# Level products of two heads issued per head on half of the array's rows, with R kept without padding

## The chip, the cores and the metric

One core of a Trainium2 chip runs the whole kernel. The metric is the device time of one execution in microseconds (us), median of the runs. Ratios are the mean time of one kernel's runs over the mean of the other's runs of the same rounds, so they are not quite the ratio of the medians quoted beside them.

## The reference, cut to what matters

A linear recurrence with a decay per step and channel feeds a layer norm and an MLP. All is float32.

```python
# r, k, v, w: (4 batches, 8 heads, 768 steps, 48 channels)
for t in range(S):
    cur = einsum('bhd,bhe->bhde', u * k[t], v[t])
    y[t] = einsum('bhd,bhde->bhe', r[t], state + cur)
    state = w[t][..., None] * state + einsum('bhd,bhe->bhde', k[t], v[t])
x = y as (4, 768, 384)
out = x + relu(layer_norm(x) @ w1) @ w2        # w1: 384 x 1536, w2: 1536 x 384
```

## The kernel before

The steps are cut into 6 chunks of 128. Inside a chunk the weight of step s in step t is built in seven levels of block sizes n = 1, 2 .. 64. At each level A = K . R over the channels gives the entries whose s lies in the left and t in the right of two sibling blocks; then K and R are multiplied by the products T of whole blocks and go to the next level. A **unit** is a pair of heads of one batch; there are 16 units, so 112 levels. The two heads share the 128 partitions, 64 each, of which 48 carry data.

R is kept twice as wide as it need be: `R[(j, d), j', t]` is zero where j' is not the partition's own head j. So one product on all 128 rows gives both heads at once, side by side in 128 columns:

```python
for lev in range(NLEV):
    n = 1 << lev; nq = HP // n; last = lev == NLEV - 1; rows = n if last else P
    ...
    for c0 in range(0, NC, CB):                      # two banks of PSUM, three chunks each
        ps = ps_a.tile([P, CB, 2 * HP], F32, ...)
        for c in range(CB):
            PE.matmul(ps[0:rows, c, :]...,           # 128 weight columns (64 in the last level)
                      a["k"][:, ds((c0 + c) * P, rows)],
                      R[:, :, ds((c0 + c) * nq, nq), 1, :], start=True, stop=True)   # 128 moving
        # VectorE copies this half into A under a mask (ScalarE in the last level)
        DVE.copy_predicated(out=to, mask=mask, data=ps)
    POOL.tensor_tensor(out=K[:, :, 0, :], in0=K[:, :, 0, :], in1=T..., op=ALU.mult)
    for j in range(2):                               # R, one head after the other, 64 partitions
        rows = ds(HP * j, HP)
        if last:
            ACT.copy(out=rs[rows, :, 0, :], in_=R[rows, j, :, 0, :])
        DVE.tensor_tensor(out=rs[...] if last else R[rows, j, :, 1, :],
                          in0=R[rows, j, :, 1, :], in1=T[rows, ...], op=ALU.mult)
    yield
```

Unit q's levels are interleaved with the end of unit q - 1, the start of unit q + 1, the conversion of the MLP weights (24 steps, VectorE mostly, during the first 24 levels) and the MLP of the batch before. So there is no MLP work until five units, 35 levels, are nearly through. Which instruction goes where between these is settled when the program is built, by a scheduler that looks at dependencies.

## Time and profile before

| | before |
|---|---|
| time, median of the first 3 runs | 800.03 us (799.59 to 804.22) |
| TensorE busy | 704 us, 88% |
| VectorE busy | 457 us, 57% |
| a level beside the MLP, first record to the MLP's next | 1.34 us |
| distance of two levels with one MLP group between them | 5.21 us |

How to read it: busy time over the whole run mixes two stages. The page's 40 slices tell them apart; the chain that ended last then says whose work the end hung on. This is the head of the chain on the page before, shares of the span by engine:

```profile
PE 76%; DVE 15%; POOL 3%; issue 3%; ACT 1%; DMA 1%; SPq 1%; POOLq 0%; ACTq 0%; DVEq 0%
```

VectorE has 15% of it, nearly all in the first 230 us.

### The profile page before, as it was taken

How to read it: one execution, taken by the hardware profiler on the slowest of the kernel's cores; microseconds unless marked ns; L12 is line 12 of the kernel's file. 1: busy time of each engine (PE TensorE's matmuls, PEld its weight loads, DVE VectorE, ACT ScalarE, POOL GpSimd, SP SyncE). 2: the span in 40 equal slices, each digit the busy share in tenths (PEclk: the TensorE clock that was granted, in tenths of full speed). 3: DMA queues.
4: the chain of work that ended last, by engine and by line, in shares of the span. 5: the costliest groups of instructions: out<-in, count | busy, mean ns of one | idle time of the engine just before them, and what ended most of it. 6: DMA issues, size and time to landing. Idle time of an engine off the chain costs nothing.

```text
span 798.1 us, 9669 instructions
## 1 busy us (share of the span) xinstructions
PE 704.1 (88%) x3640; PEld 527.0 (66%) x3640; DVE 457.0 (57%) x791; ACT 191.5 (24%) x402; POOL 258.8 (32%) x329
## 2 busy tenths in 40 slices
PE   4446665677699999999999999999999999999998
PEld 3346565567577767776867777777777776655554
DVE  5699999988964656485645555686444643200000
ACT  3034151503223122321322032212230212020110
POOL 8646564554532314141423333333121110000000
PEclk9558585859999999999999999999999999999999
DMA  9667241402310102023202020110000000000000
GB/s 155 102 139 154 64 120 60 119 5 46 75 30 16 41 20 46 0 55 70 56 1 46 21 55 1 30 35 11 1 1 11 20 1 1 20 11 11 20 1 30
DMA packets 107855, 33.86 MB, mean 42 GB/s; under 512 B 101536, under 2 KB 104736, under 8 KB 107808
## 3 DMA queue, kind: packets, MB, share of 16 engines
q1 hardware_dynamic: 107808, 33.24, 19.7%
q8 instruction: 29, 0.48, 0.2%
q14 instruction: 18, 0.15, 0.1%
HBM read 28.51 MB, written 4.72 MB: 42 GB/s over the span
## 4 chain that ended last, share of the span: by engine, by line
PE 76%; DVE 15%; POOL 3%; issue 3%; ACT 1%; DMA 1%; SPq 1%; POOLq 0%; ACTq 0%; DVEq 0%
PE h_ps L390 24%; PE o_ps L400 23%; PE a_ps L269 18%; DVE R L293 5%; PE y L338 4%; DVE A L281 3%; PE y L343 2%; POOL tot L232 2%; PE kv L315 1%; DVE we L184 1%; DVE wm L188 1%; PE k_ps L210 1%; DVE we L176 1%; PE r_ps L210 1%; DVE wm L192 1%
## 5 line engine op out<-in xcount | busy, mean ns | idle before, releaser
L269 PE MATMUL a_ps<-R,kT 128*128 128x128 f32 (+1 forms) x1344 | 198.5, 304 | 75.2 <-DVE R L293 64.5
L269 PEld LDWEIGHTS a_ps<-R,kT 128*128 128x128 f32 (+1 forms) x1344 | 186.2, 206 | 106.2 <-issue 44.1
L281 DVE COPY_PREDICATED A<-mask,a_ps 128x384 f32<-128x384 int8 x192 | 135.2, 730 | 139.1 <-PE a_ps L269 133.0
L390 PE MATMUL h_ps<-xT,w_sb 128*128 128x384 f32 x576 | 195.3, 489 | 0.5 <-ACT xT L382 0.5
L400 PE MATMUL o_ps<-w_sb,h 128*128 128x384 f32 x576 | 193.1, 487 | 0.0
L282 POOL TENSOR_TENSOR kT<-kT,tot 128x384 f32<-128x384 f32 x96 | 92.0, 958 | 257.4 <-PE a_ps L269 257.4
L400 PEld LDWEIGHTS o_ps<-w_sb,h 128*128 128x128 f32 x576 | 106.5, 190 | 67.1 <-issue 0.9
L390 PEld LDWEIGHTS h_ps<-xT,w_sb 128*128 128x128 f32 x576 | 105.6, 190 | 65.6 <-ACT xT L382 1.7
L293 DVE TENSOR_TENSOR R<-R,tot 64x384 f32<-64x384 f32 x160 | 133.4, 833 | 2.2
L406 DVE TENSOR_TENSOR o<-o_ps,x 128x384 f32<-128x384 f32 x24 | 13.4, 557 | 156.6 <-PE o_ps L400 156.6
L395 ACT ACTIVATE h<-h_ps 128x384 f32<-128x384 f32 x96 | 47.0, 490 | 149.1 <-PE h_ps L390 149.0
L338 PE MATMUL y<-v,A 128*128 128x48 f32 x384 | 56.0, 278 | 0.0
L338 PEld LDWEIGHTS y<-v,A 128*128 128x128 f32 x384 | 54.0, 207 | 0.5
L220 ACT COPY R<-r_ps 64x384 f32<-64x384 f32 x64 | 30.2, 472 | 55.3 <-PE r_ps L210 54.2
L292 ACT COPY rs<-R 64x384 f32<-64x384 f32 x32 | 16.3, 509 | 108.4 <-DVE R L293 107.9
L238 POOL TENSOR_TENSOR rk<-nat_k,nat_r 128x576 f32<-128x576 f32 x16 | 24.4, 1526 | 42.0 <-DMA nat_r<-in_r_dram 42.0
L343 PE MATMUL y<-s,rs 128*128 128x96 f32 x160 | 37.0, 316 | 0.0
L282 POOL TENSOR_TENSOR kT<-kT,wT 128x384 f32<-128x384 f32 x16 | 19.7, 1233 | 47.3 <-PE a_ps L269 47.3
L195 POOL TENSOR_TENSOR w_sb<-wm,we 128x384 f32<-128x384 f32 x24 | 27.8, 1157 | 20.4 <-DVE wm L192 14.4
L180 ACT ACTIVATE we<-we,bias 128x384 f32<-128x384 int32 x24 | 14.8, 615 | 71.3 <-DVE we L176 71.3
L232 POOL TENSOR_TENSOR tot<-tot 128x192 f32<-128x192 f32 (+4 forms) x80 | 29.4, 368 | 5.7
L343 PEld LDWEIGHTS y<-s,rs 128*128 128x128 f32 x160 | 27.2, 213 | 0.0
(59 smaller groups left out, 523.7 us busy)
## 6 DMA issues: line engine op xcount, KB each, us to landing
raw<-in_moe_w_ch_dram SPq DMA_DIRECT2D x24, 384.0 KB, 3.4
nat_w<-in_w_dram SPq DMA_DIRECT2D x32, 144.0 KB, 3.0
nat_k<-in_k_dram SPq DMA_DIRECT2D x32, 144.0 KB, 2.9
nat_r<-in_r_dram SPq DMA_DIRECT2D x32, 144.0 KB, 3.1
v<-in_v_dram SPq DMA_DIRECT2D x32, 144.0 KB, 3.6
out_dram<-o SPq DMA_DIRECT2D x24, 192.0 KB, 1.8
u_bc<-in_u_dram SPq DMA_DIRECT2D x1, 192.0 KB, 3.6
g_sb<-in_moe_g_ln_dram SPq DMA_DIRECT2D x1, 1.5 KB, 3.1
```

The lines of the kernel that those rows point to most:

```text
L195: POOL.tensor_tensor(out=dst, in0=m, in1=e.bitcast(F32), op=ALU.mult)
L220: ACT.copy(out=a["r"][rows, j, cols], in_=ps[rows])
L232: POOL.tensor_tensor(out=t, in0=pair[:, :, 0], in1=pair[:, :, 1], op=ALU.mult)
L269: PE.matmul(ps[0:rows, c, :].rearrange("s (j q n) -> s j q n", j=2, n=n), a["k"][:, ds((c0 + c) * P, rows)], R[:, :, ds((c0 + c) * nq, nq) ...
L281: DVE.copy_predicated(out=to, mask=mask, data=ps)
L282: POOL.tensor_tensor(out=K[:, :, 0, :], in0=K[:, :, 0, :], in1=T[:, :, 1][:, :, None].broadcast_to([P, S // (2 * n), n]), op=ALU.mult,)
L293: DVE.tensor_tensor(out=rs[rows, :, 1, :] if last else R[rows, j, :, 1, :], in0=R[rows, j, :, 1, :], in1=T[rows, :, 0][:, :, None].broadca ...
L338: PE.matmul(y[:, i, ts(j, D)], a_bufs[q % 2][:, c, j, :], vs[b][:, c, 2 * g + j, :], start=i + j == 0, stop=c == 0, skip_group_check=True,)
L343: PE.matmul(y[:, i, :], a["rs"][:, ts(c, P)], s[:, c - 1, :], start=False, stop=True, skip_group_check=True,)
L390: PE.matmul(ps, w1_sb[:, kc, ts(f, P)], xT[:, kc, :], start=kc == 0, stop=kc == KC - 1,)
L395: ACT.activation(out=hs[f], in_=ps, func=AF.Relu)
L400: PE.matmul(ps, hs[f][:, ts(i, P)], w2_sb[:, f, :], start=f == 0, stop=f == FC - 1)
```

## The change

The intent: do not multiply zeros. R is stored once, `[128, 768]`; each head's product uses its own half of the array's rows (48 of them) and 64 moving columns, in the hope that two heads run side by side; and one VectorE instruction on 128 partitions updates R for both. The copies of R's even halves in the last level, and half of the copies that prepare R, go away. The diff, cut to its core (the rest is renamed tiles and removed comments):

```diff
-    r_bufs = [const.tile([P, 2, S], F32, name=f"R{i}") for i in range(2)]
...
-                if nm != "r":
-                    ACT.copy(out=a[nm][:, cols], in_=ps)
-                else:
-                    for j in range(2):
-                        rows = ds(HP * j, HP)
-                        ACT.copy(out=a["r"][rows, j, cols], in_=ps[rows])
+                ACT.copy(out=a[nm][:, cols], in_=ps)
...
-            for c0 in range(0, NC, CB):
-                ps = ps_a.tile([P, CB, 2 * HP], F32, tag="a", name=f"a_ps{q}_{lev}_{c0}")
-                for c in range(CB):
+            ps = [
+                ps_a.tile([P, NC, HP], F32, tag="a", name=f"a_ps{q}_{lev}_{j}") for j in range(2)
+            ]
+            for c in range(NC):
+                for j in range(2):
+                    head = ds(HP * j, D)
                     PE.matmul(
-                        ps[0:rows, c, :].rearrange("s (j q n) -> s j q n", j=2, n=n),
-                        a["k"][:, ds((c0 + c) * P, rows)],
-                        R[:, :, ds((c0 + c) * nq, nq), 1, :],
+                        ps[j][0:rows, c, :].rearrange("s (q n) -> s q n", n=n),
+                        a["k"][head, ds(c * P, rows)],
+                        R[head, ds(c * nq, nq), 1, :],
                         start=True, stop=True,
                     )
...
-            for j in range(2):
-                rows = ds(HP * j, HP)
-                if last:
-                    ACT.copy(out=rs[rows, :, 0, :], in_=R[rows, j, :, 0, :])
-                DVE.tensor_tensor(
-                    out=rs[rows, :, 1, :] if last else R[rows, j, :, 1, :],
-                    in0=R[rows, j, :, 1, :],
-                    in1=T[rows, :, 0][:, :, None].broadcast_to([HP, S // (2 * n), n]),
-                    op=ALU.mult,
-                )
+            DVE.tensor_tensor(
+                out=R[:, :, 1, :], in0=R[:, :, 1, :],
+                in1=T[:, :, 0][:, :, None].broadcast_to([P, S // (2 * n), n]), op=ALU.mult,
+            )
```

More of the change, by code (lines that the diff above doesn't have):

```diff
@@ L136 @@
     a_bufs = [const.tile([P, NC, 2, P], F32, name=f"A{i}") for i in range(2)]
-    r_bufs = [const.tile([P, 2, S], F32, name=f"R{i}") for i in range(2)]
     kv_buf = const.tile([P, NC - 1, 2, D], F32, name="kv_sb")
-    for t in (*r_bufs, *a_bufs, kv_buf):
+    for t in (*a_bufs, kv_buf):
         DVE.memset(t, 0.0)
@@ L202, in prep @@
         b, g = units[q]
-        a = st[q] = {"r": r_bufs[q % 2]}
+        a = st[q] = {}
         for nm in "wkr":
-            if nm != "r":
-                a[nm] = p2.tile([P, S], F32, tag=nm, name=f"{nm}T{q}")
+            pool = p3 if nm == "r" else p2
+            a[nm] = pool.tile([P, S], F32, tag=nm, name=f"{nm}T{q}")
             for c0 in range(0, NC, CB):
@@ L214, in prep @@
                 cols = ds(c0 * P, CB * P)
-                if nm != "r":
-                    ACT.copy(out=a[nm][:, cols], in_=ps)
-                else:
-                    for j in range(2):
-                        rows = ds(HP * j, HP)
-                        ACT.copy(out=a["r"][rows, j, cols], in_=ps[rows])
+                ACT.copy(out=a[nm][:, cols], in_=ps)
             yield
@@ L261, in levels @@
             rows = n if last else P
-            A = a_bufs[q % 2].rearrange("s c j (q two n) -> s (c j) q two n", two=2, n=n)
-            R = a["r"].rearrange("p j (q two n) -> p j q two n", two=2, n=n)
+            A = a_bufs[q % 2].rearrange("s c j (q two n) -> s c j q two n", two=2, n=n)
+            R = a["r"].rearrange("p (q two n) -> p q two n", two=2, n=n)
             K = a["k"].rearrange("p (q two n) -> p q two n", two=2, n=n)
             T = a["T"][lev].rearrange("p (q two) -> p q two", two=2)
-            for c0 in range(0, NC, CB):
-                ps = ps_a.tile([P, CB, 2 * HP], F32, tag="a", name=f"a_ps{q}_{lev}_{c0}")
-                for c in range(CB):
+            ps = [
[4 more added lines that the diff above has]
+                    head = ds(HP * j, D)
                     PE.matmul(
-                        ps[0:rows, c, :].rearrange("s (j q n) -> s j q n", j=2, n=n),
-                        a["k"][:, ds((c0 + c) * P, rows)],
-                        R[:, :, ds((c0 + c) * nq, nq), 1, :],
+                        ps[j][0:rows, c, :].rearrange("s (q n) -> s q n", n=n),
+                        a["k"][head, ds(c * P, rows)],
+                        R[head, ds(c * nq, nq), 1, :],
                         start=True, stop=True,
                     )
-                to = A[0:rows, ds(c0 * 2, CB * 2), :, 1, :]
-                ps = ps[0:rows].rearrange("s c (j q n) -> s (c j) q n", j=2, n=n)
+            for j in range(2):
+                to = A[0:rows, :, j, :, 1, :]
+                got = ps[j][0:rows].rearrange("s c (q n) -> s c q n", n=n)
                 if last:
-                    ACT.copy(out=to, in_=ps)
+                    ACT.copy(out=to, in_=got)
                 else:
-                    mask = masks[lev][:, None].broadcast_to([P, CB * 2, nq, n])
-                    DVE.copy_predicated(out=to, mask=mask, data=ps)
+                    mask = masks[lev][:, None].broadcast_to([P, NC, nq, n])
+                    DVE.copy_predicated(out=to, mask=mask, data=got)
             POOL.tensor_tensor(
@@ L285, in levels @@
             )
-            if last:
-                a["rs"] = p2.tile([P, S], F32, tag="rs", name=f"rs{q}", bufs=1)
-                rs = a["rs"].rearrange("p (q two n) -> p q two n", two=2, n=n)
-            for j in range(2):
-                rows = ds(HP * j, HP)
-                if last:
-                    ACT.copy(out=rs[rows, :, 0, :], in_=R[rows, j, :, 0, :])
-                DVE.tensor_tensor(
-                    out=rs[rows, :, 1, :] if last else R[rows, j, :, 1, :],
-                    in0=R[rows, j, :, 1, :],
-                    in1=T[rows, :, 0][:, :, None].broadcast_to([HP, S // (2 * n), n]),
-                    op=ALU.mult,
-                )
+            DVE.tensor_tensor(
+                out=R[:, :, 1, :], in0=R[:, :, 1, :],
+                in1=T[:, :, 0][:, :, None].broadcast_to([P, S // (2 * n), n]), op=ALU.mult,
+            )
             yield
@@ L343, in tail @@
                     PE.matmul(
-                        y[:, i, :], a["rs"][:, ts(c, P)], s[:, c - 1, :],
+                        y[:, i, :], a["r"][:, ts(c, P)], s[:, c - 1, :],
                         start=False, stop=True, skip_group_check=True,
```

## The prediction

> **What bounds the kernel now.** I read the 40 slices of the page first: the run has two regimes.
>
> ```profile
> PE   4446665677699999999999999999999999999998
> DVE  5699999988964656485645555686444643200000
> PEclk9558585859999999999999999999999999999999
> ```
>
> Each digit is a slice of 20 us. Until about 225 us (slice 11) VectorE is at nine tenths and TensorE at five, at a clock that is often half; from there to the end TensorE never rests and VectorE is half idle. The table of busy times by stretch puts numbers on it (columns: stretch, its length, busy time and count of each engine, granted clock, DMA share, GB/s):
>
> ```profile
> 59.20:229.00 169.80, 116.76 (x717) 105.60 (x717) 155.02 (x277) 54.35 (x113) 89.17 (x99) 0.77 0.35 80
> 229.00:699.00 470.00, 466.20 (x2509) 342.92 (x2507) 255.40 (x447) 107.47 (x231) 131.70 (x163) 1.00 0.10 24
> ```
>
> In the first row VectorE is busy 155 of 170 us; it also converts the MLP weights there, and there is no MLP yet to give TensorE. In the second TensorE is busy 466 of 470 us: whatever a level adds to TensorE there is paid in full, and whatever it saves on VectorE is worth nothing. The last 99 us are MLP alone and the change does not touch them. Counting the levels by their start, about 37 of the 112 (16 units of 7) start before 229 us, about 75 after it.
>
> The timeline of TensorE in the full stretch shows the price of two neighbouring levels (start, length, instruction; a float32 product is two recorded matmuls, so six products are x12):
>
> ```profile
> 408.50 1.50 PE L269 MATMUL a_ps<-R,kT 128*128 128x128 f32 x12
> 409.84 4.04 PE L390 MATMUL h_ps<-xT,w_sb 128*128 128x384 f32 x12
> 413.81 1.52 PE L269 MATMUL a_ps<-R,kT 128*64 128x128 f32 x12
> 415.26 0.91 PE L390 MATMUL h_ps<-xT,w_sb 128*128 128x384 f32 x2
> ```
>
> From start to start, the first level takes 409.84 - 408.50 = 1.34 us, 0.111 us a record: that is its place in the stream. The last level of a unit has 64 weight columns in place of 128 and is no cheaper: 415.26 - 413.81 = 1.45 us, and it starts 3.97 us after the MLP group ahead of it, of which 12 x 0.3225 = 3.87 us is streaming. I come back to that 0.10 us.
>
> What bounds a record with a narrow moving side is seen in the weight loads of the output products (48 moving columns):
>
> ```profile
> 306.26 0.97 PEld L338 LDWEIGHTS y<-v,A 128*128 128x128 f32 x8
> 307.15 0.30 PEld L343 LDWEIGHTS y<-s,rs 128*128 128x128 f32 x2
> ```
>
> Eight loads take (307.15 - 306.26) / 8 = 0.111 us each, as much as a record with 128 moving columns, although 48 columns stream in under half the time. So a record here costs the larger of its streaming (0.109 us at 128 columns) and its weight load (0.111 us for 128 weight columns). In the half-clock part the same loads come every 0.213 us.
>
> [...] The trace agrees on columns (0.111 us at 128, 0.055 us between the first two loads at 64); it has no load of fewer rows. [...] the 64-column level: its first weight load waits until 0.09 us after the MLP's last streaming, instead of being loaded under it, and so does the MLP's first load after it. Together, entry and exit cost about 0.34 us (from the last MLP matmul ahead, 413.39, to the second one behind, 415.687, is 2.30 us; streaming accounts for 0.32 + 12 x 0.109 + 0.32 = 1.95). [...] The trace has 554 ns where it is undisturbed:
>
> ```profile
> L293 DVE TENSOR_TENSOR R<-R,tot x160: 540/873/1748, 24.9 to 658.9; 64x384 f32<-64x384 f32 x160
> L293 DVE TENSOR_TENSOR rs<-R,tot x32: 542/554/556, 57.6 to 660.1; 64x384 f32<-64x384 f32 x32
> ```
>
> (minimum, median and maximum in ns.) The 873 of the other levels is contention with GpSimd's multiply of K, which starts together with it[...].
>
> **The change, part by part.**
>
> R on VectorE: two instructions of 64 partitions by 384 become one of 128 by 384, at the time of one of them. The first half is the contended one, so what goes is about one undisturbed half, 0.56 us, or somewhat more where both were contended: I take 0.6 us. In the first 229 us that is 37 x 0.6 = 22 us off the engine that sets the pace.[...]
>
> ScalarE: R's preparation loses 32 of 64 copies (472 ns each, 15 us), the last level 32 copies (16 us). ScalarE is 24% busy; no gain.
>
> Copies out of PSUM: still two of 128 x 384 a level, 0.58 us undisturbed. But a head's tile is now complete only with nearly the last product, where the first half used to be complete after six of twelve records. Before the MLP starts this lengthens a level's chain by up to half a level's products (0.65 to 1.25 us), mostly under VectorE's other work. I charge 5 us, and another 5 for the TensorE cost below where it lies on the chain there: start phase -22 + 10 = -12 us.
>
> TensorE: a level goes from 6 products of 128 moving columns to 12 of 64, so 24 records; streaming stays 24 x 0.055 = 1.3 us, but the weight loads double: 24 loads of 128 columns, only on 48 rows. Two things decide: whether the loads of the two heads overlap, and the drain at each change of mode. All seven levels now work on half the rows and have full-array work around them, so all should pay the drain: 0.09 at each end, plus one exposed load (0.11) at each, plus 0.05 until the last product is through, 0.45 us in all in place of nothing.
>
> - Loads fully overlapped: 12 load times, 1.34 us, + 0.45 = 1.80, against 1.34: +0.46 us. The last level has 64 columns: 12 x 0.055 + 0.4 = 1.05 against 1.65, so -0.6 us. Over 64 ordinary and 11 last levels: 64 x 0.46 - 11 x 0.6 = +23 us.
> - Half overlapped: the records of one product [...] follow each other on the same rows and must be loaded in turn; only where the head changes can a load run beside the other. If instructions are handed out strictly in order, four records cost an estimated 0.308 in place of 0.448 us, 0.077 a record: 24 x 0.077 = 1.85, + 0.35 = 2.20, so +0.86 a level, 64 x 0.86 = 55 us, the last levels saving a little.
> - No overlap: 24 x 0.112 + 0.35 = 3.04, +1.70 us a level, 64 x 1.70 = 109 us; in the start phase at half clock a level goes from 2.55 to 5.1 us, and some 10 to 40 us come back there.
>
> With -12 us of start: 811, about 840, and 920 to 950 us.
>
> **Rivals.** First, VectorE's saving wins: if tiles overlap and the mode change costs nothing, the full stretch is level or slightly better, the start saves 15 to 22, total about 780. For it speaks that VectorE is at 90% in the start; against it the 0.34 us that the 64-column level pays today. Second, TensorE's loads take the place of the saving (the last case above): for it speaks that the trace shows loads strictly one after another at 0.111 us, and each starting only after the matmul ahead of it in program order[...]. Third, the change is hidden: VectorE is not the bound for 570 of 798 us, and 20 us in the start are eaten by the longer chain: about 800. It needs TensorE to be neutral, the same condition as the first.
>
> **Range and chances.** I give the overlapped case with drains about 40%, half overlapped 25%, none 20%, the free one 15%. The middle of that mixture lies near 824 us. The range 780 to 935 leaves out the best ends of the free case and the worst of the serial one. Faster by over 2% (under 784 us) needs the free case at its better half or luck: 0.12. Within 2% (784 to 816): most of the overlapped case: 0.33. Slower: the rest, 0.55.
>
> **What would show it.** In the changed profile: R's product 112 times at 0.6 to 0.95 us, on 128 partitions, VectorE's total down by some 70 to 90 us; the full stretch (TensorE at nine tenths) begins some 10 to 15 us earlier; a level's slot in it, first record to the MLP's next matmul, grows from 1.34 to about 1.8 (overlap), 2.2 (half) or 3.0 us (none); its weight loads' starts are about 0.055, 0.077 or 0.112 us apart on average; the gap ahead of the first and behind the last is 0.09 us. I am wrong if the loads on half the rows are cheaper than their columns say, if there is no drain for row tiles, if the clock stays low longer because TensorE's work is spread differently, or if the start was bound by the chain of levels rather than by VectorE's sum.

## The result

| | before | after |
|---|---|---|
| time, median of 4 runs | 800.71 us | 825.6 us (824.66 to 829.0) |
| ratio, 95% interval | | 1.0306 (1.027 to 1.0343) |
| TensorE busy, matmul records | 704 us, 3640 | 763 us, 4984 |
| VectorE busy | 457 us | 349 us |
| unit 4's first level begins | 183.2 us | 184.2 us |
| unit 4 lasts | 27.3 us | 40.2 us |
| unit 5's fifth level begins | 236.5 us | 248.7 us |
| from there to unit 15's last level | 424.8 us | 439.1 us |
| from there to the end | 136.8 us | 136.2 us |

Executions over 1.5% slower than the fastest of the same kernel are left out of the means. The change is slower by 3.1%. The lower rows of the table come from the profiled runs: 12 us of the loss arise before the full stretch and 14 us in it. The slices of the page after the change:

```profile
PE   5568596989899999999999999999999999999998
DVE  3588986844562424254424342464333342300000
PEclk9999999999999999999999999999999999999999
```

VectorE is no longer at nine tenths through the start, as hoped. But TensorE took its place there: eight and nine tenths well before the MLP starts. The row of the granted clock stands at nine everywhere; for the start that is not a measurement, as shown below.

The same in numbers, by the milestones of the table (stretch, its length, busy time and count of TensorE's matmuls, its weight loads, VectorE, ScalarE, GpSimd; then clock, DMA share, GB/s). Before:

```profile
0.00:236.50 236.50, 150.63 (x879) 134.32 (x880) 201.57 (x342) 70.88 (x145) 132.20 (x170) 0.76 0.45 90
236.50:661.30 424.80, 421.32 (x2307) 312.44 (x2305) 241.05 (x412) 101.48 (x217) 125.76 (x158) 1.00 0.11 25
```

After:

```profile
0.00:248.70 248.70, 195.69 (x1346) 174.21 (x1346) 161.86 (x301) 58.40 (x121) 127.30 (x170) 1.00 0.42 86
248.70:687.90 439.20, 436.09 (x3172) 308.40 (x3171) 172.64 (x338) 79.83 (x177) 125.56 (x158) 1.00 0.11 25
```

In the first row VectorE fell by 40 us and TensorE rose by 45, and the stretch got 12 us longer all the same: the main bound changed engines. In the second TensorE was full and is full.

The chain that ended last says the same of the whole run; VectorE's share fell from 15% to 6%:

```profile
PE 84%; DVE 6%; POOL 3%; DMA 2%; issue 2%; ACT 1%; SPq 1%; POOLq 0%; ACTq 0%; DVEq 0%
```

**The full stretch.** TensorE's timeline after the change, an ordinary level and a unit's last one:

```profile
556.98 1.55 PE L267 MATMUL a_ps<-rT,kT 48*128 48x64 f32 x24
558.46 4.14 PE L390 MATMUL o_ps<-w_sb,h 128*128 128x384 f32 x12
562.53 0.92 PE L267 MATMUL a_ps<-rT,kT 48*64 48x64 f32 x24
563.37 2.85 PE L390 MATMUL o_ps<-w_sb,h 128*128 128x384 f32 x8
```

The two levels begin 562.53 - 556.98 = 5.55 us apart, 5.21 before: +0.34 us. All 24 records start within 1.28 us, where 24 weight loads of 128 columns one after another would need 24 x 0.112 = 2.7. The records of the trace come in pairs, one per head, 0.007 us apart, and a pair every 0.1115 us, loads and matmuls both: the two heads overlap completely. The last level of a unit is now short, 0.84 us in place of 1.45. Together a unit takes 43.8 us in place of 42.5 (units 8 and 10, between their first levels; the odd ones 42.0 in place of about 41). Of the 14 us in this stretch, a little over one comes from a single 3.4 us at half clock (487.1 to 490.5 us): the runs below with 64 rows and with fillers for unit 4, which have none, take 437.9 us for it, not 439.1.

**R on VectorE** (count, then minimum, median and maximum in ns):

```profile
L285 DVE TENSOR_TENSOR rT<-rT,tot x96: 535/552/1336, 24.3 to 688.9; 128x384 f32<-128x384 f32 x96
L285 DVE TENSOR_TENSOR rT<-rT,wT x16: 542/586/598, 16.0 to 656.6; 128x384 f32<-128x384 f32 x16
```

One instruction on 128 partitions takes the time of one on 64: a median of 552 ns here, and 542 to 558 ns for the 47 of the 160 before that no GpSimd instruction ran beside. Of the other 113, the 67 that began while GpSimd's multiply of K ran had a median of 891 ns.

**The start.** TensorE's timeline late in the start, where neither kernel has MLP work. Before:

```profile
196.28 1.58 PE L269 MATMUL a_ps<-R,kT 128*128 128x128 f32 x12 [1.00 <-DVE R L293]
198.34 0.57 PE L338 MATMUL y<-v,A 128*128 128x48 f32 x4
198.74 0.43 PE L343 MATMUL y<-s,rs 128*128 128x96 f32 x2
```

After:

```profile
210.32 0.98 PE L328 MATMUL y<-v,A 128*128 128x48 f32 x4
211.10 0.71 PE L333 MATMUL y<-s,rT 128*128 128x96 f32 x2
211.74 2.83 PE L267 MATMUL a_ps<-rT,kT 48*128 48x64 f32 x24
```

The output products (y) are the same instructions in both kernels. Four of 48 columns take 0.40 us before (198.74 - 198.34) and 0.78 us after (211.10 - 210.32). **TensorE runs at half its pace after the change**, although the clock row says full. Their weight loads come every 0.112 or every 0.213 us.

Why does the row say full? The packed trace lists stretches of granted clock, and the page counts time that no stretch covers as full. The changed kernel's first one begins at 224.25 us, and within 0.1 us of that TensorE's spacing goes from half to full pace. Before it there is no record at all. A later run ("Fillers for unit 4 alone" below) is this kernel until unit 3's last level, with the same 2.41 us a level, and its records begin at 9 us:

```profile
12.80:186.80 174.00, 130.28 (x851) 116.72 (x851) 123.53 (x226) 40.16 (x84) 91.69 (x104) 0.50 0.43 95
```

So half pace is half clock (0.50, third number from the end). By the spacing the kernel before is at full pace in 15 of the first 35 levels, all of unit 4 among them; the changed kernel is at full pace in none. Its level takes 2.41 us from first to last record there, and 1.28 later.

### The profile page after: what moved, and what is told of

The parts are those of the page before. It is cut to its first block, busy times and chain, and to the rows that moved or that the text cites. A ratio compares the mean times of both kernels' runs of the same rounds, so it can differ in the third digit from the quotient of the medians.

```text
span 824.1 us, 12169 instructions
## 1 busy us (share of the span) xinstructions
PE 763.3 (93%) x4984; PEld 562.3 (68%) x4984; DVE 349.5 (42%) x677; ACT 157.3 (19%) x338; POOL 254.1 (31%) x329
## 4 chain that ended last, share of the span: by engine, by line
PE 84%; DVE 6%; POOL 3%; DMA 2%; issue 2%; ACT 1%; SPq 1%; POOLq 0%; ACTq 0%; DVEq 0%
PE h_ps L380 23%; PE o_ps L390 23%; PE a_ps L267 21%; PE y L328 5%; PE y L333 3%; PE kv L305 3%; DVE A L280 2%; DVE rT L285 2%; PE r_ps L209 1%; PE k_ps L209 1%; DMA nat_r<-in_r_dram 1%; PE kn_ps L300 1%; PE w_ps L209 1%; DVE we L183 1%; SPq L84 1%
## 5 line engine op out<-in xcount | busy, mean ns | idle before, releaser
L267 PEld LDWEIGHTS a_ps<-rT,kT 48*128 48x128 f32 (+1 forms) x2688 | 194.6, 221 | 94.3 <-issue 49.8
L267 PE MATMUL a_ps<-rT,kT 48*128 48x64 f32 (+1 forms) x2688 | 211.2, 310 | 45.8 <-DVE rT L285 35.7
L280 DVE COPY_PREDICATED A<-mask,a_ps 128x384 f32<-128x384 int8 x192 | 128.3, 728 | 209.1 <-PE a_ps L267 209.0
L285 DVE TENSOR_TENSOR rT<-rT,tot 128x384 f32<-128x384 f32 x96 | 63.4, 660 | 40.7 <-PE a_ps L267 40.7
L328 PE MATMUL y<-v,A 128*128 128x48 f32 x384 | 64.3, 304 | 0.0
L328 PEld LDWEIGHTS y<-v,A 128*128 128x128 f32 x384 | 59.7, 226 | 2.4
L333 PE MATMUL y<-s,rT 128*128 128x96 f32 x160 | 39.7, 336 | 0.0
L277 ACT COPY A<-a_ps 64x384 f32<-64x384 f32 x32 | 13.5, 471 | 114.1 <-PE a_ps L267 114.1
L333 PEld LDWEIGHTS y<-s,rT 128*128 128x128 f32 x160 | 29.0, 226 | 0.4
L214 ACT COPY rT<-r_ps 128x384 f32<-128x384 f32 x32 | 14.3, 481 | 70.6 <-PE r_ps L209 70.6
```

What stands on the lines that cost most here:

```text
L267: PE.matmul(ps[j][0:rows, c, :].rearrange("s (q n) -> s q n", n=n), a["k"][head, ds(c * P, rows)], R[head, ds(c * nq, nq), 1, :], start=Tr ...
L280: DVE.copy_predicated(out=to, mask=mask, data=got)
L285: DVE.tensor_tensor(out=R[:, :, 1, :], in0=R[:, :, 1, :], in1=T[:, :, 0][:, :, None].broadcast_to([P, S // (2 * n), n]), op=ALU.mult,)
L328: PE.matmul(y[:, i, ts(j, D)], a_bufs[q % 2][:, c, j, :], vs[b][:, c, 2 * g + j, :], start=i + j == 0, stop=c == 0, skip_group_check=True,)
L333: PE.matmul(y[:, i, :], a["r"][:, ts(c, P)], s[:, c - 1, :], start=False, stop=True, skip_group_check=True,)
```

## The experiments

Theories of the loss in the start: (P) pace, TensorE is left at half pace because the new products work its array less densely; (C) late copies, since a head's PSUM tile is complete only with almost the last product; (V) VectorE's saving is worth nothing, as the chain of levels and not VectorE's sum set the start. For the full stretch: overlap of the heads, and a cost at each change between half-row and full-row work (a change of mode; the drain of the prediction is the 0.09 us between the last streaming and the first weight load that the 64-column level of the kernel before shows at each end). Where a stage is discussed, the numbers are from the profiled run of each kernel.

### Products alone

The products of the change on the kernel before, R as before:

```diff
-                        a["k"][:, ds((c0 + c) * P, rows)],
-                        R[:, :, ds((c0 + c) * nq, nq), 1, :],
+                        a["k"][head, ds(c * P, rows)],
+                        R[head, j, ds(c * nq, nq), 1, :],
# with the two tiles by head, and the copies by head, as in the change
```

> The change's products (per head, half of the rows, two PSUM tiles by head) on the kernel before, which keeps its padded R and its two multiplications of R on 64 partitions. If the VectorE part of the change is worth what I predicted in the start (about 20 us), this run lies at about 845 us, 20 above the changed kernel. If the start of the changed kernel is set by TensorE and the chain of levels, taking that part back costs little: 826 to 832 us.

Measured: 864.98 us, ratio 1.0773 to before (1.0719 to 1.0828), correct. That is above both expectations. A unit late in the full stretch takes 43.8 us, as in the changed kernel, though the stretch as a whole is 444.7 us in place of 439.1 (10 us of it at half clock); the start grew to 280.9 us at unit 5's fifth level, against 236.5 before and 248.7 after the change. But this run does not measure the VectorE part purely. A level's 24 records span 3.3 us in its start, against 2.41 after the change: the built program puts four or more products of head 0 ahead of head 1's, because head 0's R is ready first, and the heads then overlap only in part. Some 30 levels at 0.9 us would be up to 27 of the 32 us; that is an estimate. What follows: the products cost the start far more than the 10 us that I charged, and one R instruction for both heads also serves their alternation.

### Half of R's work left out

```diff
-                DVE.tensor_tensor(
+                if last or j == 0:
+                  DVE.tensor_tensor(
                     out=rs[rows, :, 1, :] if last else R[rows, j, :, 1, :],
```

> The kernel before without the second head's multiplication of R in six of seven levels (a wrong result on purpose): VectorE's saving of the change without its products. If VectorE's sum sets the start, about 37 x 6/7 x 0.6 = 19 us come off: 781 us. If the chain of levels sets it, half or less of that: 790 to 799 us. The full stretch should not move: 5.21 us between two levels with one MLP group.

Measured: 786.26 us, ratio 0.9787 (0.9737 to 0.9837). Its output is wrong, which doesn't matter for the time. Unit 5's fifth level begins at 224.3 us, 12 earlier than before, and the full stretch is 1.6 us shorter. So VectorE's saving is worth 14 (profiled runs) to 17 us (ratio) of the 19 expected when the products stay as they were, 12 of them in the start. Theory V is out: the start of the kernel before does hang on VectorE. Whether through its sum or because R's multiplication also lies on the chain from level to level, this run cannot say, as it shortens both.

### Late copies

The kernel before with its products alternating between the two tiles:

```diff
-            for c0 in range(0, NC, CB):
-                ps = ps_a.tile([P, CB, 2 * HP], F32, tag="a", name=f"a_ps{q}_{lev}_{c0}")
-                for c in range(CB):
+            pss = {c0: ps_a.tile(...) for c0 in range(0, NC, CB)}
+            for c in range(CB):
+                for c0 in range(0, NC, CB):
                     PE.matmul(
-                        ps[0:rows, c, :]...
+                        pss[c0][0:rows, c, :]...
```

> The kernel before with its six products alternating between the two PSUM tiles, so that both copies have to wait until the last products, as in the changed kernel. If the lost early copy is why the start did not get shorter, the start grows by half a level's products (0.65 to 1.2 us) for most of 35 levels, so 815 to 830 us in all. If the clock is the reason, the total stays within 5 us of 800, and the full stretch unchanged in both.

Measured: 802.22 us, ratio 0.9991 (0.994 to 1.0042), correct. The first copy does start later (1.34 us after the first product in the full stretch, 0.90 before), and by the interval it costs at most some 3 us. Theory C is out as the main cause; in the changed kernel itself, where VectorE is no longer the bound, it was not tested.

### Heads in turn

```diff
-            for c in range(NC):
-                for j in range(2):
+            for j in range(2):
+                for c in range(NC):
```

> The changed kernel with all six products of head 0 ahead of all six of head 1, so that no neighbours in the stream lie on different rows except at the one change of heads. If the two heads' weight loads overlapped because they alternate, loads now come every 0.11 us instead of 0.056: a level's slot in the full stretch goes from 1.485 to about 2.8 us, 64 x 1.3 = 85 us more there, and about 2 us a level in the start at half clock, 930 to 970 us in all. If the loads on half the rows are simply cheaper, nothing changes: about 826 us.

Measured: 961.17 us (one run, state unknown), correct. TensorE's timeline, a level in the full stretch:

```profile
626.62 2.50 PE L267 MATMUL a_ps<-rT,kT 48*128 48x64 f32 x24
629.06 0.77 PE L300 MATMUL kn_ps<-ident,kT 128*128 128x128 f32 x5
```

The same 24 records now take 2.44 us to the next instruction in place of 1.49. Records of one head start every 0.112 us, as in the full-row output products: a load of 128 columns takes as long with 48 rows as with 128. Only around the change of heads do six or so records overlap, head 1's first starting when nine of head 0's twelve have started. So the full overlap here comes from alternating the heads in the program.

### Wide fillers in the start, after and before

Two products of 384 columns on the full array ahead of each level in units 0 to 4, read by nobody; the first run puts them into the changed kernel, the second into the kernel before.

```diff
+            if q <= G:
+                warm = ps_m.tile([P, RN], F32, tag="m", name=f"warm{q}_{lev}")
+                for _ in range(2):
+                    PE.matmul(
+                        warm.rearrange("p (i t) -> p i t", i=TT), ident,
+                        ident[:, None, :].broadcast_to([P, TT, P]), start=True, stop=True,
+                    )
```

> The changed kernel with two float32 filler products of 384 columns on the full array (identity by identity, into a PSUM bank that the MLP does not use yet) ahead of each level's products in units 0 to 4; nobody reads them. If the start is long because TensorE stays at half its pace there (a level's 24 records take 2.41 us, against 1.28 us later), the fillers bring it to full pace: the 24 records fall to about 1.28 us in most of the 35 levels and the whole gets shorter although 35 x 1.3 = 45 us of TensorE work are added: 790 to 815 us. If pace is not the reason, the fillers cost: 840 us or more.

Measured: 813.05 us, ratio 1.0107 (1.0033 to 1.0181), correct: about 12 us less than the changed kernel, for 45 us more of TensorE work. The timeline of TensorE in its unit 1:

```profile
85.02 1.56 PE L274 MATMUL a_ps<-rT,kT 48*128 48x64 f32 x24 [0.74 <-DVE rT L292]
86.50 2.85 PE L267 MATMUL warm<-ident 128*128 128x384 f32 x8
90.38 1.55 PE L274 MATMUL a_ps<-rT,kT 48*128 48x64 f32 x24 [1.02 <-DVE rT L292]
```

A level takes 1.5 us here, not 2.8, and TensorE waits for VectorE again. The scheduler moved the fillers ahead of their place, as they depend on nothing, so that the last ran at 163 us: unit 4 had none, was at half pace throughout, and lasted 40.3 us as in the changed kernel. Unit 4 began at 172.9 us, 11 earlier than without fillers.

> The same fillers on the kernel before. If its start is set by VectorE's sum, the pace of TensorE matters little: within 10 us of 800. If pace is the hidden difference between the kernels, this one is already at full pace for a third of these levels, so it gains less than the changed kernel does, and the changed kernel with fillers comes out ahead of this one by about the 15 us that the VectorE part was worth alone, less the 14 us that the full stretch costs: level.

Measured: 797.43 us, ratio 0.9926 (0.9877 to 0.9975), correct. Full pace in 28 of 35 levels in place of 15 gains 3 us there. In the kernel before the pace hardly matters, as expected where VectorE is the bound; after the change it does. (The guess that the two would come out level was wrong, 813 against 797: unit 4 stayed slow in the first.)

### Fillers for unit 4 alone

Fillers that read K, which the scheduler cannot move ahead, in the changed kernel from unit 3's last level on:

```diff
+            wide = {(3, 6): 4, (4, 0): 4}.get((q, lev), 2 if q == G else 0)
+            if wide:
+                warm = ps_m.tile([P, RN], F32, tag="m", name=f"warm{q}_{lev}")
+                for _ in range(wide):
+                    PE.matmul(warm, ident, a["k"][:, 0:RN], start=True, stop=True)
```

> The changed kernel with wide filler products only from the last level of unit 3 to the end of unit 4, each reading K so that it cannot be moved ahead (four at the first two places, then two a level). Unit 4 is where the changed kernel lost 13 of its 12 us in the start (40.2 us long, against 27.3 before). If pace is the cause, the levels' 24 records fall from 2.41 to 1.28 us there and unit 4 gets 6 to 12 us shorter in spite of 20 us of fillers: 812 to 820 us. If the half-row products themselves are, the unit gets longer by the fillers, 835 us or more.

("13 of its 12": unit 4 grew by 13 us and began 1 us later, and the first levels of unit 5 gave 2 back.) Measured: 825.21 us, ratio 1.028, correct: no gain in total. But the unit did what pace predicts: its first six levels ran at 1.28 to 1.29 us a level, and it lasted 34.2 us in place of 40.2 with some 10 us of fillers inside (another 8 us of them lie ahead of its first level). TensorE's timeline there:

```profile
206.90 1.46 PE L268 MATMUL warm<-kT,ident 128*128 128x384 f32 x4
208.29 1.55 PE L272 MATMUL a_ps<-rT,kT 48*128 48x64 f32 x24
```

Unit 3, with those at its end and partly at half pace, grew by 7 us and took that back. So pace is a cause of unit 4's growth, and forcing it costs about as much as it gains here.

### All 64 rows, and all 128 rows

Is it the number of rows that leaves TensorE slow? First, 64 rows a head in place of 48, 16 of them zero:

```diff
-                    head = ds(HP * j, D)
+                    head = ds(HP * j, HP)
```

> The changed kernel with each head's products on all 64 rows of its half (16 of them zero) in place of 48. If the number of rows in use decided whether TensorE comes to full pace, some levels of the start would become fast and the total fall by 5 to 12 us; if only the streaming share or the narrow products decide, the total stays at 825 us within 2 us. The full stretch stays at 5.56 us between two levels either way, since a weight load goes by its columns.

Measured: 824.31 us, ratio 1.0283 (1.0218 to 1.0348), correct. Nothing moved, half pace included (2.41 us a level). That a load of 128 columns takes 0.112 us with 48 rows as with 128, the run with the heads in turn showed; at 64 columns the kernel before has 0.055 us between its first two loads.

Second, the kernel before with each product cut into one of 64 columns per head on all rows, from the padded R:

```diff
-                        a["k"][:, ds((c0 + c) * P, rows)],
-                        R[:, :, ds((c0 + c) * nq, nq), 1, :],
+                        a["k"][:, ds(c * P, rows)],
+                        R[:, j, ds(c * nq, nq), 1, :],
# with the two tiles by head, and the copies by head, as in the change
```

> The kernel before with its products cut into two of 64 columns (one per head, from the padded R) but on all 128 rows: the same number of records and of PSUM tiles as the changed kernel, without row tiles. In the full stretch the loads come one after another, 24 x 0.111 = 2.67 us a level in place of 1.34, so 75 x 1.33 = 100 us more, with no drain. For the pace: if half of the rows is what leaves TensorE slow in the start, levels come to full pace here in units 2 to 4 as in the kernel before (24 records in 2.6 us); if narrow products whose loads take longer than their streaming are, they stay at 5 us in most of the 35 levels. 915 to 960 us.

Measured: 941.12 us (one run, state unknown), correct. Two places of TensorE's timeline, the start and the full stretch:

```profile
251.35 5.35 PE L272 MATMUL a_ps<-R,kT 128*128 128x64 f32 x24 [1.63 <-DVE R L298]
...
562.77 2.79 PE L272 MATMUL a_ps<-R,kT 128*128 128x64 f32 x24
565.39 0.71 PE L315 MATMUL kn_ps<-ident,kT 128*128 128x128 f32 x5
```

The full stretch is as expected for loads one after another, 565.39 - 562.77 = 2.62 us a level. In the start most levels are at half pace, about 4.9 us; only one level or so of each of units 1 to 4 reaches 2.6 to 2.8. So full rows do not bring the pace back for products whose weight load (0.111 us) takes longer than their streaming (64 columns, 0.054 us at the 0.84 ns a column below). That fits a pace that follows how densely the array streams. It is not proof, as this kernel's levels are also longer.

The traces say more. In them the clock changes in steps of 3.41 us: the stretches of granted clock of the kernel before last 6.83, 37.55, 6.83, 3.41 us and so on, whole multiples up to the 617.8 us of the full stretch and the MLP. For each step of all 14 profiled runs I added up how long the array streams in it: 0.84 ns a column at full pace and 1.67 at half (384 columns take 0.3225 or 0.640 us), times the share of the 128 rows that the product addresses. Time before a run's first record is counted as half clock, as the spacing shows it to be (0.213 us a load in the changed kernel).

| clock in the step | share of streaming | steps | followed by full | followed by half |
|---|---|---|---|---|
| half | 0.75 or more | 121 | 115 | 6 |
| half | less | 584 | 3 | 581 |
| full | 0.375 or more | 2606 | 2599 | 7 |
| full | less | 97 | 0 | 97 |

A level of the changed kernel at half pace streams 64 x 1.67 = 107 ns in every 213, on 96 of the 128 rows: a share of 0.375 (0.36 at full pace). With 64 rows a head, or with 64 columns on all rows, it is 0.50; with the products of the kernel before, or the fillers, 1.0. So dense levels of the new form fall among the half-clock steps below 0.75, of which 3 in 584 were followed by full clock, and those of the run with 64 rows fall there too, so that it could not have shown an effect of the rows. The two bounds of the table were chosen afterwards, to split the steps of these traces, and no run was built to test them: the table is a count, not a rule. Without the weight by rows (counting only whether the array streams) 66 steps in place of 16 fall outside the large entries of the table, 21 at half clock and 45 at full.

### One more change of mode in each level

```diff
+                if c == 2:
+                    PE.matmul(
+                        ps[0][:, 5, 0:1], ident, ident[:, 0:1], start=True, stop=True
+                    )
```

> The changed kernel with one product of a single column on the full array in the middle of each level (it writes a PSUM column that a later product overwrites), so that each level changes mode twice more. If the drain and the unhidden weight loads at a change of mode make up the 0.35 us by which a level in the full stretch got longer, each level gets about another 0.4 to 0.6 us (a pair of changes, the filler's two records at 0.11 us): 75 x 0.5 = 38 us there, more in the start at half pace, 870 to 900 us in all. If changes of mode are free, about 75 x 0.2 = 15 us.

Measured: 903.77 us (one run, state unknown), correct. A level of it in the full stretch, on TensorE's timeline:

```profile
607.08 0.89 PE L267 MATMUL a_ps<-rT,kT 48*128 48x64 f32 x12
607.90 0.38 PE L274 MATMUL a_ps<-ident 128*128 128x1 f32 x2
608.21 0.89 PE L267 MATMUL a_ps<-rT,kT 48*128 48x64 f32 x12
609.03 0.65 PE L332 MATMUL y<-v,A 128*128 128x48 f32 x4
```

From the first record to the next product the level takes 609.03 - 607.08 = 1.95 us, 1.485 in the changed kernel: 0.46 us for one pair of changes and the two records of the filler. The records between did not hide it. The full stretch grew by 45 us over the changed kernel; its trace shows 27.3 us of half clock there, 3.4 in the changed kernel, which account for about 12 of them. The other 33 fit 75 x 0.46, a little under what I expected, so a change of mode is no small thing. The change of mode and the filler are not separated by this run. The start grew by 32 us, where the same costs are paid at half pace.

### Two hybrids

Since VectorE's saving pays in the start and the old products pay beside the MLP, units 0 to 3 take the changed form and all later ones the form before. The first hybrid has free fillers, the second two fillers a level that read K:

```diff
+            if q < 4:
+                ...                                   # the changed form of a level
+                for _ in range(2 + q // 2):           # second hybrid: range(2), reading K
+                    PE.matmul(warm..., ident, ident..., start=True, stop=True)
+                ...
+                if last:
+                    a["rs"] = a["r"]
+                yield
+                continue
```

> A kernel for the gain: units 0 to 3 in the changed form with free wide fillers (two a level, three in units 2 and 3), all later units in the form of the kernel before. From the runs so far: unit 4 should begin at about 173 us, as in the changed kernel with fillers (183 before), and the rest take the 615 us that it takes before: 787 to 793 us. If the order of work that the start leaves behind matters, up to 800.

Measured: 787.95 us median of 6 runs, ratio 0.9837 (0.9792 to 0.9883), correct. By the bar of 2% the verdict is open, but the whole interval lies below one. It is the only correct kernel here that beats both by more than 1%. Unit 4 begins at 168.4 us (183.2 before), and a unit in the full stretch takes 42.5 us, as before. Unit 5's fifth level begins at 224.6 us, 12 us earlier than in the kernel before: with pace mostly kept up, the start gives the 12 us that the prediction had for it, though with fillers, and with unit 4 in the old form. Fillers alone gave 3 us.

> The same with two fillers a level that read K, so that they stay beside their level. If an even spread keeps the pace better than free fillers do, 783 to 790 us; if waiting for K puts the fillers on the chain from R to the products (1.3 us a level in 28 levels, perhaps half of it hidden), 795 to 805 us.

Measured: 807.81 us median of 6 runs, two of them slow (the four fast ones 797.41 to 809.28), ratio of the fast ones 1.0006 (0.9945 to 1.0067), correct. So holding the fillers at their level lost the gain. That they stand in the way of the products behind them is my guess and not shown: the profiled run was a slow one, and I read no more from it.

## Why the prediction was right or wrong

The time, 824, lies 2 us from the measured 825.6. That is luck. It was meant as the middle of four cases, but these weighed with their chances give about 838 (and the sum for no overlap left out the start's -12: it should read about 907 to 937). The overlapped case came true, for which I had worked out 811. It was right in kind on the full stretch, 9 us too high there, and wrong on the start by 24 us.

- **VectorE's part.** Right in kind, somewhat low in size: R fell from 173.7 us to 73 (63.4 for the ordinary form, about 9 for the first level's), 0.9 us a level where I took 0.6: the halves before had a median of 873 ns, so many that went were contended ones. VectorE's total fell by 107 us, and I had said 70 to 90.
- **Overlap of the two heads' loads.** Right for the first case: 24 records start within 1.28 us, where I had worked out 1.34. I gave this 40%, an estimate, as no trace had shown two loads side by side. The two cases of partial or no overlap (the 0.077 us a record of the first was an estimate too, and no run shows it) were wrong for this order of products; running the heads in turn shows what no alternation costs.
- **Drain at each change of mode.** Right, sized a little high: two ordinary levels are 0.34 us further apart, not 0.46. This is the size of the 0.34 us that the 64-column level showed in the trace before: a cost read off one odd instruction predicted a cost that the change put into every level. The last level saved 0.52 us (4.91 us to the next unit's first level in place of 5.43), near the 0.6 worked out. The full stretch: +14 us measured, +23 predicted.
- **The start: "start phase -22 + 10 = -12 us".** This is the step that failed. Measured: +12 us. The -22 was somewhat high (alone it is worth 12 of 19 in the start, 14 to 17 in all), but not the main error. The +10 for late copies and TensorE was. Late copies cost nothing measurable on the kernel before. TensorE cost, by difference, 12 + 12 to 15 = 24 to 27 us: the stretch was no longer bound mainly by VectorE, but by a TensorE at half pace. I had named it among what would make me wrong ("if the clock stays low longer because TensorE's work is spread differently") and given it no price. What it missed is that the new products, at a share of 0.375, came to full clock in none of the first 35 levels, where the old ones came to it in 15.
- **That VectorE's busy total sets the start** fits the kernel before (12 of 19 us in the start) and ceased to be right with the change. A saving on the bound is worth only as much as the next bound lies behind it.

How the 24 to 27 us divide is not settled exactly. Pace is shown: fillers take 11 us out of units 0 to 3, and 6 out of unit 4 net of themselves. The mode changes at half pace are shown to cost (an extra pair a level adds 32 us to the start, filler included). The two overlap, so they do not simply add. Why the new products leave TensorE slow is read from the count above, over 14 traces, and from the fillers, which bring the pace back; the bounds of that count were not tested.

## What to carry to other kernels

Two products on separate halves of the rows overlapped completely here when they alternated in the program (24 records within 1.28 us, against 2.44 us to the next instruction with the heads in turn), so splitting a packed product in two cost the streaming nothing; but entering and leaving such work cost together 0.34 us, so it should serve long runs of such products and not a dozen records between two MLP groups. When a change takes work off the bound of a stage, price the engine that comes next in that stage, and take its pace there from the spacing of instructions that both kernels share; a clock row can say full where nothing was recorded. Products that stream little can leave TensorE at half clock for a whole stage, as here (a share of 0.375, half pace in all of the first 35 levels). Different stages may want different forms of the same step: the hybrid is faster than either kernel, by 1.6% than the one before.

## What else the traces measured

- Going into the 64-column level of the kernel before and out of it costs together 0.34 us at full pace (2.297 us from the last MLP matmul ahead to the second one behind, of which 1.953 are streaming); the first weight load comes 0.09 us after the last streaming at each end, and it is not hidden. The half-row levels of the changed kernel show the same 0.34 us as added distance.
- Matmuls of the two heads on separate halves of the rows start 7 ns apart, and their weight loads too. That holds where the heads alternate: in turn, only some six of 24 records overlapped.
- Weight loads of 128 columns come 112 ns apart at full pace and 213 at half pace, with 48 rows (a pair of the two heads each time) as with 128.
- The changed kernel's TensorE worked from 142.5 to 153.8 us, no two starts more than 0.35 us apart, and stayed at half pace: work without a longer pause did not bring the full clock here.
- The records of the clock hold here wherever they exist: in all of 15,270 pairs of neighbouring 384-column matmuls of the 14 traces (each pair within one stretch of granted clock) the spacing is that of the clock on record, 0.3225 us at full and 0.640 us at half. What misled was their absence: a run can have none before its first change (at 224.25 us in the changed kernel), and its mean then counts the start as full. That is why two runs of the changed kernel with means of 0.998 and 0.871 differ by 1 us; 0.871 works out to (1 - 0.871) x 823 x 2 = 212 us at half clock, the whole start.
